# Reordering the first microseconds of a fused attention and feed-forward kernel: normalization on VectorE, values third, small weight pieces on ScalarE's queue

## The chip, the cores and the metric

The kernel runs on one core of a Trainium2 chip. The metric is the device time of one execution in microseconds (us). A core has TensorE (matrix products, with a separate path for loading weights), VectorE, ScalarE, GpSimd and SyncE; in the profile they are PE (its weight loads PEld), DVE, ACT, POOL and SP. The engines run on their own and wait for each other by semaphores. SyncE here only issues DMA transfers between the chip's main memory and the on-chip memory (SBUF). Products are written to PSUM, which has eight banks.

## The reference

All inputs are bfloat16; x has 2048 rows of 448. The computation, cut to what matters:

```python
xn = _layernorm(x)                        # rows of 448, eps 1e-5
q  = (xn @ wq)                            # 16 heads of 256
k, v = last 512 rows of the caches        # 8 heads, each used by two q heads
p  = softmax(q @ k.T * 256 ** -0.5)
s  = concat_heads(p @ v) @ wo
g  = silu((gelu(xn @ w_gate) * (xn @ w_up)) @ w_down)   # 448 -> 1792 -> 448
out = x + s * g
```

## The kernel before

The 2048 rows are worked in four chunks of 512, and each chunk in four tiles of 128 rows. A recorder (`Rec.op`) takes every operation with what it reads and writes, keeps the program order of each engine, and adds semaphore waits where data cross engines. Nothing is scheduled beyond that: the order in which the code calls the helpers is the order on each engine.

The stages are: a preamble for the first chunk; the feed-forward gate and up products of all four chunks (`gate_up`, 14 blocks of 128 columns to a chunk, line 469), each followed by the down product (line 493); then attention over 64 pairs of chunk and head (scores line 549, values line 571, output projection line 601), with the projections of q made in bursts (line 469 too). The normalization of the later chunks runs beside the feed-forward products.

The change is in the preamble, which covers the first 11 us or so:

- SyncE issues the loads in program order: the four x tiles of the first chunk (`load_x0`), the last head's values (`load_v7`), the rows 384 to 447 of gate and up for the first blocks (`load_gu6(0, 3)`: two pieces of 48 KB), the last head's part of wo (`load_wo7`), the first slice of gate and up (`load_gu(0)`: 288 KB each), the other rows 384 to 447 (`load_gu6(3, NF)`), the second slices, the x rows of the second chunk, the third slices, w_down and the rest of x. All of them have line 250 in the profile. `cuts` says where the slices of the 14 blocks end.
- TensorE makes products of a zeroed tile that nothing reads (`warm`, line 341). It transposes the last head's values (`fold_tr`, line 388), which ScalarE copies out of PSUM (`fold_copy`, line 394); then `fold(j)`, line 400, multiplies them with the last head's part of wo, for four tiles of keys, two products each. The four results, vw, are copied to SBUF by `fold_copied` (lines 407 on ScalarE and 409 on VectorE). They let the last head skip a step later.
- For each of the first four tiles VectorE takes mean and variance (`ln_stats`, lines 329 and 330), ScalarE the square root (`ln_std`, line 367), VectorE the reciprocal (line 371); then the tile is normalized (`ln_first`). Tiles 0 and 1 are normalized on ScalarE (line 375), with a bias that VectorE prepares (nmr, line 373); tiles 2 and 3 on VectorE (`ln_norm`, line 333). TensorE transposes the normalized tile (`ln_tr`, lines 351 and 353) into bank 6 or 7, and `ln_copy` brings it to SBUF as xnT: tiles 0 and 1 on ScalarE (line 364), tiles 2 and 3 on VectorE (line 362).

The first `gate_up` needs all four tiles of xnT, the first slices of gate and up, and banks 0 and 1. On TensorE the program order of the preamble is: 40 warm products, the transposes of the values, 10 warm products, tiles 0 and 1, `fold(0)`, `fold(1)`, tile 2, `fold(2)`, tile 3, `fold(3)`.

Of the kernel before, what the change touches and what calls it, by code (L numbers as in the profile page):

```python
# [5 lines left out]
ACT = mybir.ActivationFunctionType  # L6
ALU = mybir.AluOpType
BF16 = mybir.dt.bfloat16
F32 = mybir.dt.float32

LN_EPS = 1e-5
P = 128
# [132 lines left out]
def bass_recurrent_scan__sliding_block_cached__geglu_ffn__prompt_kernel(nc, A_x, A_k, A_v, A_wq, A_wo, B_x, B_wg, B_wu, B_wd, out):  # L145
    _, S, D = A_x.shape
# [5 lines left out]
    QC, TPC, HP, KF = 512, 4, 64, 3  # L152
    NQC = S // QC
    NT = NQC * TPC
    NF, NJ, NE = F // P, W // P, Dh // P
    NO = Hq * NE
    assert S % QC == 0 and D == KF * P + HP and NE == 2 and NJ == 4 and Hq == 2 * Hkv and Hq % 4 == 0 and NF % 2 == 0
    scale = float(Dh) ** -0.5
# [3 lines left out]
    with es:  # L162
        off = [16512]

        def sb(name, shape, dt, at=None):
            n = 4 if dt == F32 else 2
            for x in shape[1:]:
                n *= x
            if at is None:
                at = off[0]  # L170
                off[0] += (n + 31) // 32 * 32
            return R.place(name, shape, dt, at), at + (n + 31) // 32 * 32

        ident, _ = sb("ident", [P, P], BF16)
        small, _ = sb("small", [P, 4], F32)
        stats, _ = sb("stats", [P, NT, 6], F32)
        mv, _ = sb("mv", [P, NT, 2], F32)
        std, _ = sb("std", [P, NT], F32)
        rstd, _ = sb("rstd", [P, NT], F32)
        nmr, _ = sb("nmr", [P, 2], F32)  # L180
        den, _ = sb("den", [P, 16], F32)
        rden, _ = sb("rden", [P, 16], F32)

        xnT, _ = sb("xnT", [P, NQC, KF + 1, QC], BF16)
        gy, _ = sb("gy", [P, NT, D], BF16)
        kT, _ = sb("kT", [P, Hkv, NE, W], BF16)
        V, _ = sb("V", [P, NJ, Hkv, Dh], BF16)

        wq, _ = sb("wq", [P, KF, Hq, Dh], BF16)
        wq6, _ = sb("wq6", [P, Hq // 2, Dh], BF16)  # L190
        wo, _ = sb("wo", [P, Hq * NE, D], BF16)

        vw, _ = sb("vw", [P, NJ, D], BF16)
        gu_at = off[0]

        wg, _ = sb("wg", [P, KF, F], BF16)
        wu, _ = sb("wu", [P, KF, F], BF16)
        wgu6, x_at = sb("wgu6", [P, F], BF16)
        x4, _ = sb("x4", [P, NT, D], BF16)
        NX = 4  # L200
        xn2, d_at = sb("xn2", [P, NX, D + HP], BF16)
        wd, _ = sb("wd", [P, NF, D], BF16)
# [42 lines left out]
        act = lambda *a, **k: R.op("scalar", *a, **k)  # L245
        dve = lambda *a, **k: R.op("vector", *a, **k)
        pool = lambda *a, **k: R.op("gpsimd", *a, **k)

        def dma(eng, dst, src, w=(), r=(), after=(), lane=None):
            return R.op(eng, lambda e: e.dma_start(dst, src), r=r, w=w, dma=True, after=after, lane=lane)  # L250

        def dmaT(dst, src, w=(), r=(), after=(), lane=None):
# [9 lines left out]
             r=[("ident",)], w=[("ident",)])  # L262


        def load_x0(a, b):
            dma("sync", x4[:, a:b, :], x_view[:, 0, a:b, :], w=[("x4", t) for t in range(a, b)])

        w_gu = [(w, name, src[0:KF * P, :].rearrange("(k p) n -> p k n", p=P), src[KF * P:D, :])
                for w, name, src in ((wg, "wg", B_wg), (wu, "wu", B_wu))]
        cuts = [0, 3, 8, NF]  # L270
        jslice = {j: s for s in range(3) for j in range(cuts[s], cuts[s + 1])}

        def load_gu(s):
            a, b = cuts[s] * P, cuts[s + 1] * P
            for w, name, src, _ in w_gu:
                dma("sync", w[:, :, a:b], src[:, :, a:b], w=[(name, s)])

        def load_gu6(a, b):

            for h, (_, name, _, src) in enumerate(w_gu):  # L280
                dma("sync", wgu6[h * HP:(h + 1) * HP, a * P:b * P], src[:, a * P:b * P], w=[("wgu6", h, a > 0)])

        def load_x(c):
            dma("sync", x4[:, c * TPC:(c + 1) * TPC, :], x_view[:, c, :, :],
                w=[("x4", c * TPC + t) for t in range(TPC)])
# [5 lines left out]
        def load_v7():  # L291
            dma("sync", V[:, :, Hkv - 1, :], v_view[:, :, Hkv - 1, :], w=[("V", "f")])

        def load_wo7():
            dma("sync", wo[:, NO - NE:NO, :], wo_v[:, NO - NE:NO, :], w=[("wo", "f")])

        for t in range(TPC):
            load_x0(t, t + 1)
        load_v7()
        load_gu6(0, 3)  # L300
        load_wo7()
        load_gu(0)
        load_gu6(3, NF)
        load_gu(1)
        load_x(1)
        load_gu(2)
        dma("sync", wd[:, :, :], B_wd.rearrange("(f p) d -> p f d", p=P), w=[("wd",)])
# [20 lines left out]
        def ln_stats(t):  # L328
            dve(lambda e: e.bn_stats(stats[:, t, :], x4[:, t, :]), r=[("x4", t)], w=[("stats", t)])
            dve(lambda e: e.bn_aggr(mv[:, t, :], stats[:, t, :]), r=[("stats", t)], w=[("mv", t)])  # L330

        def ln_norm(t, eng=dve):
            eng(lambda e: e.tensor_scalar(xn2[:, t % NX, 0:D], x4[:, t, :], mv[:, t, 0:1], rstd[:, t:t + 1],
                                          op0=ALU.subtract, op1=ALU.mult),
                r=[("x4", t), ("mv", t), ("rstd", t)], w=[("xn2", t % NX, 0)])

        def warm(n):

            def run(e):
                for _ in range(n):  # L340
                    ins = e.matmul(bank(3, P), lhsT=actT[:, NF - 1, 0:P], rhs=actT[:, NF - 1, 0:P], start=True, stop=True)  # L341
                return ins
            pe(run, r=[("actT", NF - 1)], w=[("ps", 3)])

        def ln_tr(t):
            b = 6 + t % 2
            tp = bank(b).bitcast(BF16)

            def tr(e):
                for k in range(KF):  # L350
                    e.transpose(tp[:, k * P:(k + 1) * P], xn2[:, t, k * P:(k + 1) * P], ident[:, :])  # L351
                for lo in (0, HP):
                    ins = e.transpose(tp[lo:lo + HP, KF * P:(KF + 1) * P], xn2[:, t, KF * P:D], ident[:, :])  # L353
                return ins
            pe(tr, r=[("xn2", t, 0), ("ident",)], w=[("ps", b)])

        def ln_copy(t):
            b = 6 + t % 2
            dst = xnT[:, 0, :, t * P:(t + 1) * P]
            src = bank(b).bitcast(BF16)[:, 0:(KF + 1) * P].rearrange("p (k q) -> p k q", q=P)  # L360
            if t >= 2:
                dve(lambda e: e.tensor_copy(dst, src), r=[("ps", b)], w=[("xnT", 0, t)])  # L362
            else:
                act(lambda e: e.activation(dst, src, ACT.Copy), r=[("ps", b)], w=[("xnT", 0, t)])

        def ln_std(t):
            act(lambda e: e.activation(std[:, t:t + 1], mv[:, t:t + 1, 1], ACT.Sqrt, bias=small[:, 0:1]),
                r=[("mv", t), ("eps",)], w=[("std", t)])

        def ln_first(t):  # L370
            dve(lambda e: e.reciprocal(rstd[:, t:t + 1], std[:, t:t + 1]), r=[("std", t)], w=[("rstd", t)])
            if t < 2:
                dve(lambda e: e.scalar_tensor_tensor(nmr[:, t:t + 1], mv[:, t, 0:1], -1.0, rstd[:, t:t + 1], op0=ALU.mult, op1=ALU.mult),
                    r=[("mv", t), ("rstd", t)], w=[("nmr", t)])
                act(lambda e: e.activation(xn2[:, t, 0:D], x4[:, t, :], ACT.Identity, bias=nmr[:, t:t + 1], scale=rstd[:, t:t + 1]),
                    r=[("x4", t), ("nmr", t), ("rstd", t)], w=[("xn2", t, 0)])
            else:
                ln_norm(t)


        vT = actT[:, NF - 3:NF - 1, :]
# [11 lines left out]
        def fold_copy():  # L393
            act(lambda e: e.activation(vT.rearrange("p m k -> p (m k)"), bank(0).bitcast(BF16), ACT.Copy),
                r=[("ps", 0)], w=vT_keys)

        def fold(j):
            def run(e):
                for m in range(NE):
                    ins = e.matmul(bank(2 + j, D), lhsT=vT[:, m, j * P:(j + 1) * P], rhs=wo[:, NO - NE + m, :],  # L400
                                   start=m == 0, stop=m == NE - 1)
                return ins
            pe(run, r=vT_keys + [("wo", "f")], w=[("ps", 2 + j)])
# [5 lines left out]
                dve(lambda e: e.tensor_copy(vw[:, j, :], bank(2 + j, D)), r=[("ps", 2 + j)], w=[("vw", j)])  # L409


        warm(40)
        fold_tr()
        for a in range(0, TPC, 2):
            for t in (a, a + 1):
                ln_stats(t)
                ln_std(t)
            for t in (a, a + 1):
                ln_first(t)
            if a == 0:  # L420
                fold_copy()
        warm(10)
        for t in range(2):
            ln_tr(t)
            ln_copy(t)
        fold(0)
        fold(1)
        ln_tr(2)
        ln_copy(2)
        fold(2)  # L430
        ln_tr(3)
        ln_copy(3)
        fold(3)
        fold_copied(0, act)
        fold_copied(1, dve)
        fold_copied(2, dve)
# [212 lines left out]
        for c in range(NQC):  # L649
            lead = 6 if c == 0 else 2  # L650
            for f in range(NF + 1):
# [4 lines left out]
                t = (f - lead) // 2  # L656
# [25 lines left out]
        for i in range(NI):  # L682
            for t in range(TPC):
# [5 lines left out]
                if t % 2 == 0 and early:  # L689
                    n = n_pieces(outs[1][0])  # L690
# [3 lines left out]
                if 7 <= i and t % 2 and not (i >= Hq and i % Hq == 6):  # L694
                    n = n_pieces(outs[0][0])
# [48 lines left out]
```

## Time and profile before

| | us |
|---|---|
| median of 3 runs (lowest, highest) | 559.02 (558.72, 559.38) |
| the profiled execution | 559.23 |
| its span | 557.4 |
| first gate product (line 469) starts | 11.03 |
| TensorE busy in the span | 550.0 (99%) |

The span runs from the first to the last instruction that the profiler recorded; the profiled execution's own time is 1.83 us longer. Starts are counted from the beginning of the span. A row of a group or of the timeline gives the line of the kernel, the engine, the operation, what it writes and reads, and how often; "idle before" names what ended the engine's idle time, by the semaphores that the profiler saw.

### The profile page before, as it was taken

Reading aid. Unit: us, or ns where it says so; the run is one execution under the profiler, and the core shown is the slowest. Engines: PE = TensorE matmul, PEld = TensorE weight load, DVE = VectorE, ACT = ScalarE, POOL = GpSimd, SP = SyncE. Lnnn points to the kernel's source line nnn. Section 1 sums busy time; section 2 is a strip of 40 time slices with the busy share of each in tenths; the row PEclk is TensorE's granted clock in tenths of the full one; section 3 lists DMA queues with packets and bytes.
Section 4 is the critical chain, followed back from the end, with each engine's and each line's share of the span. In section 5 each row is a group of like instructions: output and inputs, shape, how many; then the busy total and the mean of one; then the engine's idle time right before and its main releaser. Section 6 shows DMA issues by size and latency. Waiting matters only on the chain.

```text
span 557.4 us, 9904 instructions
## 1 busy us (share of the span) xinstructions
PE 550.0 (99%) x3523; PEld 263.1 (47%) x3556; DVE 313.2 (56%) x822; ACT 297.2 (53%) x690; POOL 88.4 (16%) x125
## 2 busy tenths in 40 slices
PE   8999999999999999999999999999999999999997
PEld 6554444444444444444444444444444444444445
DVE  5544427043463578177718753772688077628774
ACT  5433324237656665555575556546665655575640
POOL 0131213200000111002301110131121002311134
PEclk9999999999999999999999999999999999999999
DMA  8862554952544355245545551467355255635552
GB/s 233 286 147 67 129 90 84 223 155 59 102 89 76 51 102 96 58 85 93 130 72 96 102 96 39 97 93 143 66 96 100 43 86 101 134 70 104 95 96 52
DMA packets 164640, 57.65 MB, mean 103 GB/s; under 512 B 155616, under 2 KB 161504, under 8 KB 164592
## 3 DMA queue, kind: packets, MB, share of 16 engines
q1 hardware_dynamic: 161408, 44.81, 42.9%
q0 software_dynamic: 3040, 12.16, 8.1%
q8 instruction: 28, 0.46, 0.4%
q14 instruction: 20, 0.16, 0.1%
q10 hardware_dynamic: 144, 0.06, 0.0%
HBM read 17.92 MB, written 1.84 MB: 35 GB/s over the span
## 4 chain that ended last, share of the span: by engine, by line
PE 98%; issue 1%; DMA 1%; DVE 0%; SPq 0%
PE ps L469 33%; PE ps L549 20%; PE ps L571 19%; PE ps L601 18%; PE ps L493 8%; DMA V<-in_A_v_cache_dram 1%; SPq L250 0%; PE ps L400 0%; PE ps L388 0%; PE ps L351 0%; PE ps L353 0%; PE ps L341 0%; DVE vw L409 0%; DVE xnT L362 0%; DVE tmp L612 0%
## 5 line engine op out<-in xcount | busy, mean ns | idle before, releaser
L553 ACT ACTIVATE pr<-ps 128x512 bf16<-128x512 f32 x256 | 152.6, 598 | 120.1 <-PE ps L549 118.9
L549 PE MATMUL ps<-kT,qT 128*128 128x512 bf16 x487 | 145.3, 379 | 2.3 <-issue 1.4
L555 DVE RECIPROCAL rden<-den 128x1 f32<-128x1 f32 x256 | 41.3, 161 | 154.2 <-ACT pr L553 139.6
L571 PE MATMUL ps<-pT,V 128*128 128x512 bf16 x472 | 121.9, 379 | 0.4
L556 DVE TENSOR_SCALAR pr<-pr,rden 128x512 bf16<-128x512 bf16 x256 | 106.0, 414 | 9.0
L601 PE MATMUL ps<-wo,oT 128*128 128x448 bf16 (+1 forms) x498 | 110.9, 346 | 0.0
L469 PE MATMUL ps<-xnT,wq 64*128 64x512 bf16 x896 | 98.2, 376 | 0.0
L524 ACT ACTIVATE qT<-ps 128x1024 bf16<-128x1024 f32 x64 | 64.5, 1023 | 43.4 <-PE ps L469 43.0
L469 PE MATMUL ps<-xnT,wg 64*128 64x512 bf16 x336 | 81.8, 376 | 0.8 <-DVE vw L409 0.8
L469 PE MATMUL ps<-xnT,wu 64*128 64x512 bf16 x336 | 82.5, 376 | 0.0
L578 DVE CAST oT<-ps 128x512 bf16<-128x512 f32 x118 | 80.5, 682 | 0.7 <-PE ps L571 0.6
L487 DVE TENSOR_TENSOR actT<-ps,hb 128x512 bf16<-128x512 f32 x56 | 38.5, 692 | 66.7 <-ACT hb L486 62.5
L549 PEld LDWEIGHTS ps<-kT,qT 128*128 128x128 bf16 x512 | 49.2, 98 | 55.4 <-issue 4.0
L571 PEld LDWEIGHTS ps<-pT,V 128*128 128x128 bf16 x480 | 46.9, 98 | 56.3
L601 PEld LDWEIGHTS ps<-wo,oT 128*128 128x128 bf16 x498 | 48.4, 98 | 48.6 <-DVE acc L624 1.0
L469 PEld LDWEIGHTS ps<-xnT,wq 64*128 64x128 bf16 x896 | 43.0, 94 | 54.6 <-DVE rden L555 1.7
L486 ACT ACTIVATE hb<-ps 128x512 bf16<-128x512 f32 x56 | 33.1, 594 | 39.0 <-PE ps L469 38.9
L553 ACT ACTIVATION_READ_ACCUMULATOR pr<-ps 128x1 f32 x256 | 50.2, 196 | 0.0
L493 PE MATMUL ps<-wd,actT 128*128 128x448 bf16 x224 | 46.2, 353 | 0.0
L469 PEld LDWEIGHTS ps<-xnT,wg 64*128 64x128 bf16 x336 | 31.3, 94 | 20.6 <-DVE vw L409 1.2
L643 POOL TENSOR_SCALAR tmp<-tmp 128x448 f32<-128x448 f32 x16 | 9.0, 562 | 198.4 <-ACT tmp L642 198.4
L469 PEld LDWEIGHTS ps<-xnT,wu 64*128 64x128 bf16 x336 | 31.3, 94 | 19.2
(62 smaller groups left out, 265.7 us busy)
## 6 DMA issues: line engine op xcount, KB each, us to landing
pT<-pr SPq DMA_TRANSPOSE x240, 2.5
wq<-in_A_wq_dram POOLq DMA_DIRECT2D x14, 256.0 KB, 3.6
wo<-in_A_wo_dram POOLq DMA_DIRECT2D x3, 896.0 KB, 8.7
V<-in_A_v_cache_dram POOLq DMA_DIRECT2D x4, 448.0 KB, 7.4
xr<-in_A_x_dram POOLq DMA_DIRECT2D x4, 448.0 KB, 4.4
wd<-in_B_w_down_dram SPq DMA_DIRECT2D x1, 1568.0 KB, 12.7
x<-in_A_x_dram SPq DMA_DIRECT2D x3, 448.0 KB, 7.6
out_dram<-xr POOLq DMA_DIRECT2D x3, 448.0 KB, 3.3
```

What stands on the lines that cost most here:

```text
L469: ins = e.matmul(bank(s + m)[:, q0:q1], lhsT=lhsT, rhs=xnT[lo:lo + HP, c, k, q0:q1], start=ph == 0 and k == 0, stop=ph == 1 and k == KF - 1)
L486: act(lambda e: e.activation(hb[:, h, :], bank(s), ACT.Gelu_apprx_tanh), r=[("ps", s)], w=[("hb", h)])
L487: dve(lambda e: e.tensor_tensor(actT[:, f, :], bank(s + 1), hb[:, h, :], ALU.mult), r=[("ps", s + 1), ("hb", h)], w=[("actT", f)])
L493: pe(lambda e, f=f: e.matmul(bank(b, D), lhsT=actT[:, f, t * P:(t + 1) * P], rhs=wd[:, f, :], start=f == 0, stop=f == NF - 1), r=[("actT", ...
L524: act(lambda e: e.activation(buf[:, :, e_, :], psum[:, s * 512:(s + 2) * 512].rearrange("p (a q) -> p a q", a=2), ACT.Copy), r=[("ps", s), ...
L549: ins = e.matmul(bank(b), lhsT=buf[:, a, k, t * P:(t + 1) * P], rhs=kT[:, g, k, :], start=k == 0, stop=k == NE - 1)
L553: act(lambda e: e.activation(pr[s][:, :], bank(b), ACT.Exp, scale=scale, accum_out=den[:, s:s + 1]), r=[("ps", b)], w=[("pr%d" % s,), ("de ...
L555: dve(lambda e: e.reciprocal(rden[:, s:s + 1], den[:, s:s + 1]), r=[("den", s)], w=[("rden", s)])
L556: dve(lambda e: e.tensor_scalar(pr[s][:, :], pr[s][:, :], rden[:, s:s + 1], None, op0=ALU.mult), r=[("pr%d" % s,), ("rden", s)], w=[("pr%d ...
L571: ins = e.matmul(bank(b), lhsT=V[:, j, g, e_ * P:(e_ + 1) * P], rhs=src[:, j, :], start=j == 0, stop=j == NJ - 1)
L578: dve(lambda e: e.tensor_copy(dst, bank(b)), r=[("ps", b)], w=[key])
L601: ins = e.matmul(bank(b, D)[:, lo:hi], lhsT=lhsT, rhs=rhs, start=idx == 0, stop=idx == n8 - 1)
```

## The change

ScalarE no longer normalizes tiles 0 and 1: VectorE does it for all four, and the bias nmr is gone. The last head's values are loaded third, ahead of x tiles 2 and 3. The two small pieces of gate and up are issued by ScalarE. The second slices have four blocks instead of five, the third seven instead of six, and gate's second slice is loaded ahead of the rest of rows 384 to 447. There are 32 and 4 warm products instead of 40 and 10. On TensorE the eight `fold` products all stand between tile 1 and tile 2. On VectorE each of tiles 2 and 3 is finished (reciprocal, normalization, copy after the transposes) before the next begins, and the copies of tiles 0 and 1 on ScalarE stand between the square roots of tiles 2 and 3.

```diff
-        nmr, _ = sb("nmr", [P, 2], F32)
...
-        cuts = [0, 3, 8, NF]
+        cuts = [0, 3, 7, NF]
...
+        def load_w(n, s):
+            a, b = cuts[s] * P, cuts[s + 1] * P
+            w, name, src, _ = w_gu[n]
+            dma("sync", w[:, :, a:b], src[:, :, a:b], w=[(name, s)])
+
         def load_gu(s):
-            a, b = cuts[s] * P, cuts[s + 1] * P
-            for w, name, src, _ in w_gu:
-                dma("sync", w[:, :, a:b], src[:, :, a:b], w=[(name, s)])
-
-        def load_gu6(a, b):
+            load_w(0, s)
+            load_w(1, s)
+
+        def load_gu6(a, b, eng):
 
             for h, (_, name, _, src) in enumerate(w_gu):
-                dma("sync", wgu6[h * HP:(h + 1) * HP, a * P:b * P], src[:, a * P:b * P], w=[("wgu6", h, a > 0)])
+                dma(eng, wgu6[h * HP:(h + 1) * HP, a * P:b * P], src[:, a * P:b * P], w=[("wgu6", h, a > 0)])
...
-        for t in range(TPC):
+        for t in range(2):
             load_x0(t, t + 1)
         load_v7()
-        load_gu6(0, 3)
+        for t in range(2, TPC):
+            load_x0(t, t + 1)
         load_wo7()
+        load_gu6(0, 3, "scalar")
         load_gu(0)
-        load_gu6(3, NF)
-        load_gu(1)
+        load_w(0, 1)
+        load_gu6(3, NF, "sync")
+        load_w(1, 1)
         load_x(1)
         load_gu(2)
...
         def ln_first(t):
             dve(lambda e: e.reciprocal(rstd[:, t:t + 1], std[:, t:t + 1]), r=[("std", t)], w=[("rstd", t)])
-            if t < 2:
-                dve(lambda e: e.scalar_tensor_tensor(nmr[:, t:t + 1], mv[:, t, 0:1], -1.0, rstd[:, t:t + 1], op0=ALU.mult, op1=ALU.mult),
-                    r=[("mv", t), ("rstd", t)], w=[("nmr", t)])
-                act(lambda e: e.activation(xn2[:, t, 0:D], x4[:, t, :], ACT.Identity, bias=nmr[:, t:t + 1], scale=rstd[:, t:t + 1]),
-                    r=[("x4", t), ("nmr", t), ("rstd", t)], w=[("xn2", t, 0)])
-            else:
-                ln_norm(t)
+            ln_norm(t)
...
-        warm(40)
+        warm(32)
         fold_tr()
-        for a in range(0, TPC, 2):
-            for t in (a, a + 1):
-                ln_stats(t)
-                ln_std(t)
-            for t in (a, a + 1):
-                ln_first(t)
-            if a == 0:
-                fold_copy()
-        warm(10)
+        for t in range(2):
+            ln_stats(t)
+            ln_std(t)
+        for t in range(2):
+            ln_first(t)
+        fold_copy()
+        warm(4)
         for t in range(2):
             ln_tr(t)
+        for j in range(NJ):
+            fold(j)
+        for t in range(2, TPC):
+            ln_stats(t)
+            ln_std(t)
+            ln_copy(t - 2)
+        for t in range(2, TPC):
+            ln_first(t)
+            ln_tr(t)
             ln_copy(t)
-        fold(0)
-        fold(1)
-        ln_tr(2)
-        ln_copy(2)
-        fold(2)
-        ln_tr(3)
-        ln_copy(3)
-        fold(3)
         fold_copied(0, act)
```

## The prediction

> **What bounds the kernel now.** I read the page first, for the engine that sets the time: the busy row of section 1 and the chain of section 4.
>
> ```profile
> PE 550.0 (99%) x3523; PEld 263.1 (47%) x3556; DVE 313.2 (56%) x822; ACT 297.2 (53%) x690; POOL 88.4 (16%) x125
> PE 98%; issue 1%; DMA 1%; DVE 0%; SPq 0%
> ```
>
> TensorE carries 98% of the chain. The change touches only what runs before the first gate product (line 469), so its worth is the shift of that product's start, called T0, plus any hole that new loading order makes later. Next I read the chain in order of time for the first 30 us (start, length, what; all in us), to find T0 and what is ahead of it.
>
> ```profile
> 2.59 2.87 DMA V<-in_A_v_cache_dram
> ...
> 5.51 0.86 PE ps L388 x8
> 6.37 0.56 PE ps L341 x10
> ...
> 7.72 0.86 PE ps L400 x4
> ...
> 9.80 0.42 DVE xnT L362
> 10.23 0.54 DVE vw L409
> 10.77 0.26 issue
> 11.03 19.15 PE ps L469 x175
> ```
>
> T0 is 11.03, and from there TensorE has no hole for 19 us. The chain blames a vw copy (line 409), but that first gate product does not read vw, nor the banks that line 409 empties. It reads the normalized tiles, whose last copy ends at 9.80 + 0.42 = 10.22, and the first slices of wg and wu. So I looked at the DMA view of the first 40 us (size, median us from issue to landing).
>
> ```profile
> wg<-in_B_w_gate_dram SPq DMA_DIRECT2D x1, 288.0 KB, 3.2
> wu<-in_B_w_up_dram SPq DMA_DIRECT2D x1, 288.0 KB, 5.4
> V<-in_A_v_cache_dram SPq DMA_DIRECT2D x1, 256.0 KB, 2.9
> wo<-in_A_wo_dram SPq DMA_DIRECT2D x1, 224.0 KB, 3.0
> ```
>
> The timeline has wu's first slice issued at 5.45; it lands at 5.45 + 5.4 = 10.85, 0.15 before the first weight load at 11.00. That is the last wait now. Were wu early, T0 would be 10.22 plus the 0.19 that VectorE's result needs to start a product (normalization of tile 2 ends 8.24, its transpose starts 8.43): 10.41. So removing the wu wait alone is worth at most 0.62 us.
>
> **The change part by part.** The order of issue on SP first. An issue takes 0.42 to 0.6, and the small gate/up pieces took 0.57 and 0.59. V takes the third place, that of x tile 2, so it is issued at 1.65 instead of 2.59; x tiles 2 and 3 go 0.47 later each; wo's piece moves from 4.31 to about 3.06, wg's first slice from 4.94 to 3.7, wu's from 5.45 to 4.2. With wu's landing bounded by the two 288 KB rows (3.2 and 5.4), it lands between 7.4 and 9.6. That wait leaves the path.
>
> The two small pieces go to ScalarE, which is idle from 2.23 to 3.73, when the first square root starts. Two issues cost 2 x 0.59 by SP's rows, or 2 x 0.37 by the one issue that ScalarE makes in this trace, at the end; they are over by 3.4, which hides them. If they took twice as long, the square roots would slip about 1 us, and the normalization of tile 0 (needed at about 6.0, ready at 4.9) would just be late.
>
> VectorE's normalization: two ScalarE rows of 0.75 and two bias rows of 0.16 go; two VectorE rows of 0.40 come. Reciprocals at 4.34 and 4.85, normalized tiles at 4.93 and 5.44 instead of 6.17 for the second. Queued behind them on VectorE are the statistics of tile 2: 0.62 + 0.18 and 0.59 + 0.18 from 5.40, done near 7.0; then reciprocal and normalization, so tile 2 is ready near 7.6 (8.24 before).
>
> Now TensorE's program order decides: warm-up 32, transposes of V, warm-up 4, tiles 0 and 1, all eight vw products, tile 2, tile 3. V lands at 1.65 + 2.87 = 4.52 by its own row; with the small pieces' 96 KB fully ahead of it, at the 239 to 264 KB per us that the windows from 3 to 5 us show, it is 0.4 later, 4.9. I take 4.6, since most of those packets start after V's. [...]
>
> From V's landing to the vw products: the transposes start 0.05 later and the copy of V (line 394) starts 0.95 after the landing (5.46 to 6.41) and takes 1.02, so it ends at 4.6 + 1.97 = 6.57; the products start 0.19 later, 6.75. wo's piece, 3.06 + 3.0 = 6.06, is there; tiles 0 and 1 are transposed by then if their products run at the later pace (2 x 0.35 after 6.0). Eight products, 2 x 0.86 = 1.72, end at 8.47.
>
> Behind that end stands a tail that is now serial, because VectorE copies tile 2 before it takes the reciprocal of tile 3. From rows: last vw product to copy of tile 2, 0.39 (9.41 to 9.80); copy 0.42; reciprocal and normalization of tile 3, 0.51; hand to TensorE 0.19; transposes to copy 0.54 (8.43 to 8.97); copy 0.42; hand to TensorE 0.19. Sum 2.66. T0 = 8.47 + 2.66 = 11.13, against 11.03: +0.10. Before, tile 3 was normalized beside tile 2's transposes and the third vw product, and only one tile and two products followed; so the time that the loads give back is spent in this order.
>
> Tile 2's own readiness (7.6) is hidden by the products (8.47). If that cover were gone, T0 would be 7.6 + 0.19 + 0.54 + 0.42 + 0.51 + 0.19 + 0.54 + 0.42 + 0.19 = 10.6, the least I can build. At the other end, V at 4.9 adds 0.3, and tiles 0 and 1 at the early pace (10 x 0.107 from 6.0) hold the products until 7.07, +0.3: 11.7.
>
> After T0: a gate block takes 1.51 (line 486 starts 13.62, 15.13, 16.64), so block f starts at T0 + 1.51 f - 0.65. Block 3 wants wu's second slice at 15.0; it landed at 7.79 + 6.9 = 14.69, and is now smaller and issued near 6.5, so about 13.4. Block 7 now wants the third slices, at 21.0; they landed at 17.7 and 19.2, with the same bytes ahead in sum, so 1.8 us covers them; with that gone TensorE would wait there. The x loads and all work beyond are issued no later. Nothing else is on the path.
>
> **Sum.** The profiled execution took 559.23 (span 557.4 and 1.83 around it), so 559.33 by the same account. It lies 0.21 over the median of the runs shown, 559.02; some of those may have had wu earlier. I say 559.2.
>
> **The rivals.**
>
> *The clock comes later (slower).* The first 40 warm-up products take 4.18 for 40 weight loads, 0.105 each, and V's eight transposes 0.86, 0.107 each; the ten after them take 0.56, 0.056 each. So TensorE doubles its pace near 6.2, some 5.2 after its first product, although the page's granted clock shows 9 in every slice.
>
> ```profile
> 0.97 4.18 PEld L341 LDWEIGHTS ps<-actT 128*128 128x128 bf16 x40 [0.97 <-DVE actT L256]
> 5.51 0.86 PE L388 MATMUL ps<-ident,V 128*128 128x128 bf16 x8
> 6.21 0.72 PE L341 MATMUL ps<-actT 128*128 128x128 bf16 x10
> ```
>
> The change cuts 14 of these 50 products and may open gaps at V's landing and ahead of the vw products. If the doubling came a further 5.2 after a restart at 6.75, the vw products would run at 0.43 each from 7.07, end at 10.5, and T0 would be about 13.2: 561.3. It costs over 1.1 us once the doubling is later than about 8.2. For it: less work to keep TensorE busy. Against: the old gap of 0.35 at 5.16 didn't prevent it, nor did the later gap of 0.8 lose it. [...] Chance 0.11.
>
> *The products do not gate (a little faster).* If the eight products start earlier (TensorE at its later pace already for V's transposes, 0.4 less) T0 is 10.6 to 10.7: 558.8. For it: the pace may change in another place of each run. Against: this execution's rows. Chance 0.13.
>
> *Every tile moves (either side).* Removing nmr, 32 bytes, moves all later tiles from multiples of 64 bytes to 32 past one. No row shows a TensorE operand at such an address. A third of a nanosecond on each of 3523 products would be 1.1 us; one whole nanosecond makes 562.7. Nothing in the trace speaks for it. Chance 0.05.
>
> **How the numbers follow.** My case (T0 10.8 to 11.8) has 0.71, own range 558.7 to 559.9. The range 558.4 to 560.5 adds the earlier T0, and the lower part of a late clock. A difference within 0.2%, 1.1 us, is about what a measurement of this kernel can tell from no change. Faster than that needs T0 below 9.9, which no chain here gives; I leave 0.07 for the moved tiles and what I don't see. Slower: the clock 0.11, tiles and a late slice 0.06. The rest, 0.76, is the same.
>
> **What would show it.** Right: V's transposes (line 388) near 4.6; the eight products of line 400 in one piece from 6.75 to 8.5; the copies of line 362 near 8.9 and 10.5, more than 1.5 apart (0.83 before); the first line 469 near 11.1 and wu landed by 9.6. Wrong: line 469 released by a wg or wu landing, line 400 at 0.43 each, a hole in line 469 near 15 or 21, or a different mean for the 512-column products later on.

## The result and the profile after

The changed kernel takes 561.46 us (median of 17 runs, 560.22 to 564.04), the kernel before 559.21 (17 runs, 558.51 to 560.23). The ratio is 1.0046, 95% interval 1.0033 to 1.0058: 2.25 us slower at the median. The profiled execution took 562.36 (span 560.6), 3.13 more than the one of before.

The spread is part of the result. Nine of the 17 runs have a mean granted clock below 1.0 (0.997 or 0.994), and their median is 562.15; the other eight show 1.0, median 560.79; below, such runs are called undisturbed. Of 72 later runs of the kernel before none was under 0.999. A 1.0 has to be read with care: the trace's clock record begins only where the pace of TensorE first doubles (at 6.05 before, at 6.17 here), and three of the traces below have no record at all, so a late rise doesn't lower the mean. The slowest of the 17 runs, 564.04, shows 1.0, and what it met isn't known.

Page of the changed kernel: the busy row, the engines of the chain, and the group of the q products (line numbers after the change are one lower for most of the kernel; each experiment's edit shifts them again).

```profile
PE 550.7 (98%) x3509; PEld 261.2 (47%) x3542; DVE 313.8 (56%) x822; ACT 295.9 (53%) x688; POOL 88.6 (16%) x125
PE 97%; DMA 1%; issue 1%; SPq 0%; DVE 0%
L468 PE MATMUL ps<-xnT,wq 64*128 64x512 bf16 x896 | 98.2, 376 | 0.0
```

The q products take 98.2 us at 376 ns each, as on the page of before. So the long part of the kernel runs as it did, although all large tiles moved by 32 bytes: the loss is in the first 17 us. The chain in order of time (start, length, what) shows the first half of it.

```profile
3.44 4.83 DMA wo<-in_A_wo_dram
8.27 0.14 issue
8.41 1.67 PE ps L400 x8
10.08 0.17 PE ps L357 x3
...
10.47 0.42 DVE xnT L368
...
11.00 0.41 DVE xn L339
...
11.45 0.34 PE ps L357 x3
...
12.01 0.44 DVE xnT L368
12.45 0.05 issue
12.49 23.01 PE ps L468 x196
```

wo's piece lands at 8.27, and everything to the first gate product hangs on it: eight vw products, then tile 2 and tile 3 one after the other. T0 is 12.49 instead of 11.03, +1.46. The second half is in the windows view. Its columns are the window in us, its length, then busy time of PE, PEld, DVE, ACT and POOL, then the granted clock, the DMA share and GB/s. The bounds are where the trace's clock record begins or changes (6.17, 12.99 and 16.41) and points 3.41 from there: that is the length of the stretch at half clock, and the one at full clock ahead of it is twice as long, 6.82.

```profile
6.17:9.58 3.41, 2.28 (x22) 1.34 (x20) 1.60 (x6) 2.96 (x7) 0.00 (x0) 1.00 0.99 315
9.58:12.99 3.41, 1.86 (x19) 0.96 (x19) 1.87 (x6) 1.45 (x2) 0.00 (x0) 1.00 1.10 264
12.99:16.41 3.42, 3.42 (x20) 1.25 (x18) 1.04 (x2) 0.00 (x0) 0.00 (x0) 0.50 1.04 383
16.41:19.82 3.41, 3.41 (x36) 1.51 (x34) 1.38 (x2) 1.22 (x3) 0.00 (x0) 1.00 1.07 353
```

From 12.99 to 16.41 TensorE gets half its clock: 20 products fall into that window and 36 into the next. That costs half of 3.41, 1.7 us. The two halves, 1.46 + 1.7 = 3.16, account for the 3.13 by which the profiled execution is longer.

Why wo is late begins with the first 7 us of the timeline of the changed kernel:

```profile
0.73 1.28 ACT L290 ACT_TABLE_LOAD   x1 [0.73 <-PEq L728]
0.86 0.58 ACTq L249 DMA_DIRECT2D wgu<-in_B_w_gate_dram  x1
1.48 0.61 ACTq L249 DMA_DIRECT2D wgu<-in_B_w_up_dram  x1
...
3.97 0.63 DVE L335 BATCH_NORM_STATS2 stats<-x 128x6 f32<-128x448 bf16 x1 [0.37 <-DMA x<-in_A_x_dram]
...
5.19 1.03 PE L388 MATMUL ps<-ident,V 128*128 128x128 bf16 x8 [0.61 <-DMA V<-in_A_v_cache_dram]
...
6.98 0.63 DVE L335 BATCH_NORM_STATS2 stats<-x 128x6 f32<-128x448 bf16 x1 [0.43 <-DMA x<-in_A_x_dram]
```

ScalarE issues the small pieces at 0.86 and 1.48, while its activation table is still loading. They share the DMA engines with what SyncE loads: by the DMA view of 2 to 4 us, SyncE's queue had 61.9% of the 16 engines' time and moved 0.34 MB, theirs 21.2% and 0.10 MB; the run below that has them on SyncE moved 0.50 in all. The last statistics wait for x tile 3 until 6.98; they started at 5.81 before. By the DMA view wo's piece needs 4.8 from issue to landing, 3.0 before.

### The profile page after: what moved, and what is told of

Same layout as the page of the kernel before. It is cut to its first block, busy times and chain, and to the rows that moved or that the text cites. A ratio compares the mean times of both kernels' runs of the same rounds, so it can differ in the third digit from the quotient of the medians.

```text
span 560.6 us, 9872 instructions
## 1 busy us (share of the span) xinstructions
PE 550.7 (98%) x3509; PEld 261.2 (47%) x3542; DVE 313.8 (56%) x822; ACT 295.9 (53%) x688; POOL 88.6 (16%) x125
## 3 DMA queue, kind: packets, MB, share of 16 engines
HBM read 17.92 MB, written 1.84 MB: 35 GB/s over the span
## 4 chain that ended last, share of the span: by engine, by line
PE 97%; DMA 1%; issue 1%; SPq 0%; DVE 0%
PE ps L468 33%; PE ps L548 19%; PE ps L570 18%; PE ps L600 18%; PE ps L492 8%; DMA wo<-in_A_wo_dram 1%; SPq L249 0%; PE ps L400 0%; DVE xnT L368 0%; PE ps L357 0%; DVE xn L339 0%; DVE tmp L611 0%; DVE xr L613 0%; PE ps L359 0%; DVE rstd L377 0%
## 5 line engine op out<-in xcount | busy, mean ns | idle before, releaser
L468 PE MATMUL ps<-xnT,wq 64*128 64x512 bf16 x896 | 98.2, 376 | 0.0
L468 PE MATMUL ps<-xnT,wg 64*128 64x512 bf16 x336 | 83.4, 381 | 0.5 <-DVE xnT L368 0.5
L468 PE MATMUL ps<-xnT,wu 64*128 64x512 bf16 x336 | 83.7, 381 | 0.0
```

What stands on the lines that cost most here:

```text
L468: ins = e.matmul(bank(s + m)[:, q0:q1], lhsT=lhsT, rhs=xnT[lo:lo + HP, c, k, q0:q1], start=ph == 0 and k == 0, stop=ph == 1 and k == KF - 1)
```

## The experiments

Two theories stood after the result. One: T0 is later because wo's piece lands late, behind the small pieces, and the new order puts a serial tail behind it. Two: the holes that this leaves on TensorE cost the clock. The rivals were that the shorter warm-up costs the clock, and that the second queue itself is slow.

**The small pieces back on SyncE, behind wo's piece.**

```diff
-        load_gu6(0, 3, "scalar")
+        load_gu6(0, 3, "sync")
```

> The changed kernel with the two small pieces back on SyncE, behind wo's piece. Theory 2 (on ScalarE's queue they are issued at 0.86, before V and x tile 1, and push V, x tiles 1 to 3 and wo's piece back): V lands near 4.5, wo's piece near 6.5, the vw products start near 6.8 and the first gate product near 11.3 instead of 12.5; median near 559.5 if the clock stays full, 561 where it drops. Rival (wo's piece is late because V and x stand ahead of it, or because of slow packets of its own): wo still lands near 8.2 and the first gate product stays near 12.5, 561.5.

Measured: 559.56, ratio 1.0006 (0.9997 to 1.0016) to the kernel before. From its chain:

```profile
3.14 3.72 DMA wo<-in_A_wo_dram
...
7.00 1.67 PE ps L400 x8
...
11.09 5.09 PE ps L468 x29
```

wo lands at 6.86 and T0 is 11.09, 0.36 and 0.2 off what was expected and far from the rival's. This one line takes back nearly all of the loss at the median. In the other profiles with the pieces issued first and wo's piece behind x tiles 2 and 3, wo landed between 7.67 and 8.57, so the late landing isn't one run's. Three of ten runs still lose the clock (median 560.87, the other seven 559.31).

**The pieces on ScalarE, but later.** They follow the square root of tile 1.

```diff
-        load_gu6(0, 3, "scalar")
...
+        load_gu6(0, 3, "scalar")
         for t in range(2):
             ln_first(t)
         fold_copy()
```

> The changed kernel with the two small pieces still on ScalarE's queue, but issued after the square root of tile 1 instead of as ScalarE's first work. Theory 2a (it is the moment: issued at 0.86 they stand in front of V, x tiles 1 to 3 and wo's piece): x tile 1 lands near 3.3, V near 4.5, wo's piece by 7.0, the first gate product near 11.1 and undisturbed runs near 559.3, as with SyncE's queue. [...]

Measured: 560.79, ratio 1.0027 (1.0013 to 1.0041); five of ten runs at clock 1.0, median 559.69. wo's piece lands at 7.19 and the vw products run from 7.32, so the early moment did hold wo back by about 1.1 us (theory 2a). x tile 1 still comes at 3.96 (3.90 with the pieces on SyncE, 3.3 before), so that delay isn't theirs; V, which is now loaded right behind it, is the likely cause. But a new wait decides, which theory 2a did not have. From the DMA view (KB, median us to landing) and the timeline of this kernel:

```profile
wg<-in_B_w_gate_dram SPq DMA_DIRECT2D x1, 384.0 KB, 6.9
...
wgu<-in_B_w_gate_dram SPq DMA_DIRECT2D x1, 176.0 KB, 7.2
...
wgu<-in_B_w_gate_dram ACTq DMA_DIRECT2D x1, 48.0 KB, 6.8
wgu<-in_B_w_up_dram ACTq DMA_DIRECT2D x1, 48.0 KB, 7.2
```

```profile
12.74 0.58 PE L468 MATMUL ps<-xnT,wg 64*128 64x512 bf16 x1 [1.85 <-DMA wgu<-in_B_w_up_dram]
```

The two pieces of 48 KB, issued at 4.84 and 5.42, land last of all that the first block reads, at 11.65 and 12.61. The two loads of SyncE shown were issued at 4.65 and 5.18 and landed at 11.52 and 12.37: the four land in the order of their issue, over both queues. The last section has more on it.

**The pieces on ScalarE in the kernel before**, the load order and all else unchanged.

```diff
-        load_gu6(0, 3)
+        load_gu6(0, 3, "scalar")
```

> The kernel before with one edit, the two small pieces on ScalarE's queue. By theory 2a x tiles 1 to 3 and V land later (V after 5.8 instead of 5.46), which costs up to 0.5, while wo and wu are issued 1.2 earlier; the old order of products has no serial tail and few holes: 559.2 to 559.8, clock 1.0 in nearly all runs. If the pieces on ScalarE cost 1.2 by themselves, whatever the order: 560.4 and more.

Measured: 559.45, ratio 1.0008 (0.9995 to 1.0022), no run under 1.0. V lands at 5.93 instead of 5.46, and T0 of the profiled run still comes earlier, at 10.61: wu, issued 1.07 sooner, lands at 10.38, and the chain goes from V through TensorE's program order. The old order has room for V's delay because wu's landing was its last wait. So the 1.5 us that the pieces on ScalarE cost (560.79 against 559.31 at a clock of 1.0) come only together with the new order. Four of the ten runs lie at 560.5 to 562.5 with a mean clock of 1.0; what they met is not in the one profile, which is of a quicker run.

**wo's piece ahead of x tiles 2 and 3** in the changed kernel.

```diff
-        for t in range(2, TPC):
-            load_x0(t, t + 1)
         load_wo7()
+        for t in range(2, TPC):
+            load_x0(t, t + 1)
```

> The changed kernel with wo's piece loaded ahead of x tiles 2 and 3. Theory 3 (wo's landing is what starts the vw products, and with them the serial tail): wo lands near 7.0 instead of 8.3, vw products from 7.2, first gate product 11.2 to 11.6 (x tiles 2 and 3 land about 0.8 later, tile 2 ready near 8.9), undisturbed runs near 559.6. If the vw products wait for something else (V's copy, the pieces), first gate product stays near 12.4 and undisturbed runs near 560.8.

Measured: 561.98, ratio 1.0044 (1.0026 to 1.0063). wo is early enough for the vw products to run from 7.01, and T0 in the profiled run is 11.43, inside what was expected; now x tile 2 releases the chain at 6.72. But six of eight runs lose the clock; the two others took 559.65 and 559.70. So the late vw products were wo's doing, and starting them earlier left TensorE with more idle time behind. The two windows around its drop:

```profile
7.89:11.30 3.41, 1.84 (x15) 0.76 (x12) 2.07 (x9) 3.15 (x7) 0.00 (x0) 1.00 1.06 283
11.30:14.71 3.41, 3.28 (x16) 1.20 (x18) 1.67 (x4) 0.00 (x0) 0.00 (x0) 0.50 1.07 329
```

**The old order of products and tiles**, with the loads, queues and warm-up of the change.

```diff
-        for j in range(NJ):
-            fold(j)
         for t in range(2, TPC):
             ln_stats(t)
             ln_std(t)
             ln_copy(t - 2)
         for t in range(2, TPC):
             ln_first(t)
-            ln_tr(t)
-            ln_copy(t)
+        fold(0)
+        fold(1)
+        ln_tr(2)
+        ln_copy(2)
+        fold(2)
+        ln_tr(3)
+        ln_copy(3)
+        fold(3)
```

> The changed kernel with TensorE's and VectorE's old order of products and tiles (two vw products pairs, tile 2, one, tile 3, one; tile 3 normalized before tile 2 is copied); loads, queues, VectorE's normalizations and 32 and 4 warm products as changed. Theory 3 (the serial tail of 2.66 us behind the last vw product is the price of the new order): the vw products still start near 8.4 with wo's landing, the first gate product comes near 11.1 instead of 12.5, TensorE has fewer holes and the clock stays: median near 559.4. Rival (only wo's landing counts, the order hides nothing): 12.3 and 560.5 to 561.5.

Measured: 559.86, ratio 1.0010 (0.9996 to 1.0023); the seven runs at clock 1.0 have a median of 559.29, 1.5 under those of the changed kernel. Its profiled run lost the clock already at 7.65, for two windows, so its T0 of 13.21 says nothing on the order. wo landed at 8.57 in it, late as expected. The expected T0 of 11.1 is thus not seen in a trace; the times of the undisturbed runs fit it.

**Fewer warm products in the kernel before**, 32 and 4.

> The kernel before with 32 and 4 warm products in place of 40 and 10, nothing else. If the shorter warm-up alone makes the clock late or lets it drop: over 560.5, a half clock in some runs. If the sparse stretch behind it does (theory 1): first gate product unchanged near 11.0, clock 1.0, 559.2 within 0.4.

Measured: 559.66, ratio 1.0004 (0.9994 to 1.0013), one run in ten under 1.0 (0.997). The median lies 0.06 above theory 1's range and well under its rival's 560.5, but T0 of the profiled run is 11.75, not 11.0: there the clock rose only at 9.98, a window later, and the window before 6.57, with 1.10 idle ahead of V's transposes, has TensorE busy for 2.31 of 3.41. The shorter warm-up can cost some tenths; it isn't the 2.25.

**Filling TensorE's holes**: products of the zero tile, which nothing reads, added to the changed kernel in three versions. First 16 ahead of the vw products, 14 after tile 2 and 5 after tile 3.

```diff
+        def fill_pe(n):
+            def run(e):
+                for _ in range(n):
+                    ins = e.matmul(bank(1, P), lhsT=actT[:, NF - 1, 0:P], rhs=actT[:, NF - 1, 0:P], start=True, stop=True)
+                return ins
+            pe(run, r=[("actT", NF - 1)], w=[("ps", 1)])
...
+        fill_pe(16)
         for j in range(NJ):
             fold(j)
...
             ln_tr(t)
+            fill_pe(14 if t == 2 else 5)
             ln_copy(t)
```

> The changed kernel with 35 more products of the zero tile, in TensorE's three holes (16 ahead of the vw products, 14 after tile 2's transposes, 5 after tile 3's). Theory 1 (a sparse TensorE between 7 and 12.5 us makes the clock drop to half for one or two windows of about 3.4 us, which costs about 1.6 us each): granted clock 1.0 in all runs, first gate product still near 12.5, median near 560.6, spread under 1 us. Rival (the drop comes from the shorter warm-up ahead of 6 us, or is chance): half clock after 13 us stays in about half of the runs, median near 561.5.

Measured: 561.70 in five runs, all at 1.0. No drop shows, but T0 was 13.61: V came at 5.39, the pace doubled only near 9.2, and the 16 products, most of them at the slow pace, took about 1.5 and themselves pushed the vw products from wo's landing, 8.0, to 9.5. Inconclusive on the sum. Second, only in the tail, 10 and 6:

> The changed kernel with 16 more products of the zero tile, only in the two holes behind the vw products (10 after tile 2's transposes, 6 after tile 3's), where they fit into the idle time at the full pace. Theory 1 (the holes of the serial tail leave a window of 3.4 us too idle, and the clock drops after it): runs with a mean clock under 1.0 go from 9 in 17 to at most 1 in 10, the first gate product stays near 12.5, the median falls from 561.5 to 560.5 to 560.8. Rival (the drop is decided by the gaps ahead of 8.4 us): about half of the runs still under 1.0, median 561.3 to 561.7.

Measured: 561.43, two of five runs under 1.0. Five runs are few, but two drops are more than the at most one in ten that was expected. So the holes of the tail alone don't decide the drop; theory 1 as written there fell, and had to take in the gaps ahead of the vw products. Third, dense from the start:

```diff
-        warm(32)
+        warm(42)
...
+        fill_pe(10)
         for j in range(NJ):
             fold(j)
...
             ln_tr(t)
+            fill_pe(12 if t == 2 else 6)
             ln_copy(t)
```

> The changed kernel with TensorE kept busy from the first warm product to the first gate product: 42 warm products (they reach to V's landing near 5.2), then 10 products of the zero tile ahead of the vw products and 12 and 6 in the tail. Theory 1 in its later form (the clock follows the busy share of free-running windows of 3.41 us: in the eight traces so far it rose after windows busy 2.80 or more and not after 2.59 or less, and fell after 1.87 or less and not after 2.28 or more): every window above 2.9, the clock full by 6.5 and never lost, first gate product near 12.5, all runs 560.2 to 561.2, median 560.7; so 1.4 of the loss stays and the clock's part goes. If dense products don't decide it: runs under a mean clock of 1.0 again, median 561.4.

Measured: 560.44, ratio 1.0020 (1.0011 to 1.0028), all 11 runs at 1.0 and between 559.92 and 560.88. Its chain has the first gate product at 12.07, and its windows are filled. This trace has no clock record; the windows start at 4.20, where the products go from 0.107 apart to 0.056:

```profile
4.20:7.61 3.41, 3.13 (x46) 2.44 (x44) 3.19 (x12) 2.13 (x6) 0.00 (x0) 1.00 0.93 236
7.61:11.03 3.42, 2.79 (x25) 1.75 (x26) 0.89 (x3) 2.55 (x5) 0.00 (x0) 1.00 1.06 296
11.03:14.44 3.41, 3.33 (x33) 1.70 (x35) 2.02 (x4) 0.00 (x0) 0.00 (x0) 1.00 1.08 330
```

The middle window is 2.79, not above 2.9 as expected. With TensorE kept busy the drops are gone (none in 11 runs, against nine in 17), and 1.2 of the 2.25 stays (560.44 against 559.28 in the same comparison): the later T0, which no filling mends. That leaves about 1.1 for the clock. The split isn't sharp. T0 in this profile is 0.42 earlier than in the changed kernel's, as wo landed at 7.85; and the changed kernel's own runs at a clock of 1.0 lie 1.6 over the kernel before (560.79 against 559.21), which leaves the clock 0.7.

**Both repairs together**: the pieces on SyncE, the old order, 34 and 6 warm products.

> What the experiments point to: the changed kernel with the small pieces back on SyncE behind wo's piece, the old order of vw products and tiles, and 34 and 6 warm products. wo's piece near 6.9, vw products from there, tile 3 copied near 10, so the first gate product waits for wu's landing (9.5 to 10.5): 10.3 to 10.7, 558.5 to 558.9, clock 1.0 in nearly all runs; the kernel before 559.4. If the tail of tile 3 still gates, 11.0 and 559.4.

Measured: 559.08 against 559.32, ratio 0.9994 (0.9985 to 1.0003), no run under 1.0. It isn't told from the kernel before, and misses the expected 558.5 to 558.9. Tile 3 is copied by 9.93, and then TensorE waits for wu, issued at 5.47 with 5.3 to landing, 10.8:

```profile
wu<-in_B_w_up_dram SPq DMA_DIRECT2D x1, 288.0 KB, 5.3
```

```profile
10.93 0.37 PE L472 MATMUL ps<-xnT,wg 64*128 64x512 bf16 x1 [0.98 <-DVE vw L409]
```

Either repair alone brings undisturbed runs to 559.3. The second adds 0.2, which isn't clear of the noise; in the profiled run T0 is 10.93, and the loads bound the start again. No version here beats the kernel before clearly.

## Why the prediction was wrong

- *wu leaves the path.* Right in effect: it landed at 10.2 (4.44 + 5.8), not by 9.6, and still ahead of T0. The view that T0 was its landing, not a vw copy, is borne out by the kernel before with the pieces on ScalarE, where wu came earlier and T0 with it (10.61).
- *ScalarE's two issues.* Wrong. I put them after 2.23, behind the table load, and so "most of those packets start after V's". They went at 0.86 and 1.48, and landed at 3.29 and 4.34, ahead of V. SyncE's own issues stretched beside them: x tiles 2 and 3 took 1.16 for two, 0.98 with the pieces on SyncE, and wo's issue came at 3.44 rather than 3.06 (3.14 with the pieces on SyncE).
- *V lands at 4.6.* It landed at 5.14, outside my 4.9. With them first it was 5.07 to 5.39 in the five profiles of this load order, without them 4.70, 4.76 and 5.08. So part of the miss is V's own, and how much is theirs stays open.
- *"wo's piece, 3.06 + 3.0 = 6.06, is there."* This is the term that failed. It was 3.44 + 4.83 = 8.27. I had bounded V and wu from both sides and taken wo's duration from a single row, and I had charged the small pieces' 0.4 to V alone: for wo they were put at nothing. The same 224 KB took 3.0 from issue to landing before, 4.83 here and 3.72 with the pieces behind them on SyncE, so one row was no measure of the landing. With the pieces behind it wo landed 1.41 earlier, at 6.86; their bytes (0.4 at the prediction's rate) and the later issue (0.30) make half of that, and the other half stays open. The miss moved the start of the vw products from 6.75 to 8.41, +1.66.
- *Eight products 1.72, serial tail 2.66.* Measured 1.67 and 2.41 (10.08 to 12.49). These held, and T0 would have been near 11.1 with wo on time: with the pieces on SyncE it was 11.09.
- *The clock comes later* (chance 0.11). The rise came at 6.17, 0.12 after that of before. What happened was the other edge: the full clock was lost at 12.99, behind a window whose idle time, 1.03 and 0.53, is that of the serial tail in my own sum. I had argued that the gap of 0.8 did not lose it before. That gap lay in a window with 2.63 of 3.41 busy, shown here, and the lost one has 1.86. The rival's 561.3 lies near the result by luck: it had the slow pace on the vw products, 0.43 each, which ran at 0.21, and I tied it to the warm-up, which the 40-to-32 edit alone does not bear out.

```profile
9.46:12.88 3.42, 2.63 (x25) 1.26 (x24) 2.02 (x4) 1.25 (x2) 0.00 (x0) 1.00 1.03 289
```

- *Every tile moves.* Ruled out for the q products: 376 ns in both.
- *Later slices.* Right: no hole from 12.49 to 35.5.

The range ended at 560.5; the runs with a full clock alone (560.79) would already have left it. A range that had put wo's landing at the length that the DMA view gave for wu (5.4) would have allowed a T0 of 3.06 + 5.4 + 0.15 + 1.72 + 2.66 = 13.0, or 561.1: enough for the undisturbed runs, but the median of 561.46 needs the lost clock as well, which the sum did not have.

## What to carry to other kernels

Cost a landing by all that is issued ahead of it, on every queue; a row of the old order is no bound once the order changes (wo's 3.0 became 3.6 to 5.1 over the runs, wu's 5.4 became 4.8 to 6.8). When a reordering leaves the busiest engine waiting in short gaps, add up its busy time over the stretches in which the clock is seen to change (3.41 us here), since small gaps can cost more than their own length: here 1.03 and 0.53 stood ahead of a half clock that cost another 1.7. And a tail that is serial by one engine's program order passes every late load in front of it on in full: either repair, the load or the order, was enough here for the undisturbed runs.

## What the runs showed of the hardware

**The clock changed in steps of 3.41 us, and with the busy time of TensorE in the step before.** In the changed kernel the clock record shows full clock for 6.82 (6.17 to 12.99) and half for 3.42 (to 16.41); in the run with the old order of products full for 3.41 (4.24 to 7.65) and half for 6.83 (to 14.48). The steps lie at another moment in each run (the rise came at 4.24, 4.47, 5.16, 5.32, 6.04, 6.05 or 6.17, and at 8.92 and 9.98 where the window before it ended without a rise). Ahead of the rise no record shows the steps: there the windows are counted back from it by 3.41, and half clock means the slow pace, 0.107 from product to product against 0.056 behind the rise (before and changed). Busy time of TensorE per window, over the profiled runs above that have the record:

| at the window's end | busy us of 3.41 |
|---|---|
| full clock kept | 2.28 (changed), 2.43 (both repairs), 2.62, 2.63 (before), 2.76, 2.98 and more |
| full clock lost | 1.13, 1.84, 1.86 (changed), 1.87, 1.87 |
| half clock ends | 2.80 (changed), 2.82 (pieces later), 3.07 and more |
| half clock stays | 2.31 (fewer warm products), 2.35, 2.59 (tail filled) |

So in these traces the clock fell behind windows busy 1.87 or less and behind none busy 2.28 or more, and rose behind windows busy 2.80 or more and behind none busy 2.59 or less. What happens in between, they don't show. The longest gap doesn't order them: the changed kernel's window from 6.17, which kept the clock, holds one of 1.13, and the one after it, which lost it, 1.03 at most. Busy time is modelled by the profiler, so the bounds are the profile's.

**Transfers landed in the order of their issue, over both queues.** In each of the eight profiles with the pieces on ScalarE the first 19 transfers landed in the order in which the two engines issued them, whatever their size. So 48 KB on ScalarE's queue took 2.4 and 2.9 when issued first of all, and 6.8 and 7.2 when issued into a loaded SyncE queue. In the second case the packets came late: by the DMA view ScalarE's queue moved one packet from 5 to 8 us, beside 1091 of SyncE's, and the other 159 from 8 to 12. What held them until then is open.

**ScalarE's queue issued while its table loaded**: in the changed kernel at 0.86 and 1.48, inside the load from 0.73 to 2.01.
